# Two list fetches per slot instead of up to five in a row, and one if with an else at the end, in a fused attention and mixture-of-experts kernel

## The chip, the cores and the metric

The kernel runs on 1 core of one Trainium2 chip. The metric is the device time of one execution in microseconds (us). The engines are called as the profile calls them: PE (TensorE matmul), PEld (its weight load), DVE (VectorE), ACT (ScalarE), POOL (GpSimd) and SP (SyncE).

## The reference

Block-sparse attention over q, k and v of shape 4 x 8 x 768 x 64, then a mixture of eight experts in which each of the 3072 tokens goes to one expert:

```python
k_sum = k.reshape(B, H, nb, block, D).max(axis=3)          # 24 blocks of 32
v_sum = v.reshape(B, H, nb, block, D).mean(axis=3)
# softmax over the keys nearer than 16 and the 24 block sums (score + log 32)
a = softmax([local scores, summary scores])
x = (a @ [v, v_sum]) -> [3072, 512]
logits = x @ w_gate;  e_idx = argmax(logits)
for e in range(8):
    mask = e_idx == e
    ye = np.maximum(x[mask] @ w1[e], 0.0) @ w2[e]           # 512 -> 1024 -> 512
    out[mask] = gate_w[mask, None] * eom[mask, e, None] * ye
```

`gate_w` is the softmax probability of the chosen expert and `eom` the sigmoid of `x @ w_output_gate`.

## The kernel before, in words

**Attention and routing.** `attention` (L177) goes through 48 stages: 4 batches, 6 tiles of 128 tokens, 2 groups of 4 heads. PE transposes keys and queries, forms the scores (L329), transposes the probabilities (L347) and multiplies them with the values (L358); DVE and ACT do the softmax between them. Each finished tile `xs` of x (DVE, L368) is stored to DRAM (`x_dr`) by POOL (L371). When a batch is through, its 768 tokens are routed (L401 to L460): DVE works out for every token its expert, its weight and its place in that expert's list, and POOL scatters the pairs (token number, weight) into the lists in DRAM, `l_dr`, with six indirect DMAs for each batch, one for each tile (L456). Every scatter is remembered in `rt["scatters"]`.

**Slots.** The experts' lists are cut into slots of 256 tokens of one expert. For a slot POOL issues three kinds of indirect DMAs, two of each (128 tokens each):

- the *list fetch* (`fetch_list` L751, issued at L757) brings 256 pairs from `l_dr` into a tile of its own. It waits for all scatters that were issued up to then;
- the *row fetch* (`fetch` L765, L770) gathers the rows of x that the list names into the tiles `xg`, of which there are only two, so it can start when PE has transposed the rows of the slot before;
- the *write* (`write` L923; DVE L929, ACT L931, POOL L932) scatters the scaled results to the output.

`take_x` (L794) transposes the rows (PE L803) and splits them into two parts of lower precision (ACT L805, DVE L806). `first` (L813) is the first layer, 8 times 12 matmuls (L821 to L823), then ReLU and split (L824, L825). `second` (L913) is the second layer, 8 blocks of 6 matmuls (L909 to L911); ahead of its fifth block it takes the rows of the next slot and issues the row fetch of the one after. `fetch_w` (L774) loads the weights of the next slot (SP L789) and splits them (ACT L791, DVE L792). `half` (L855) handles a slot of 128 tokens.

**Order of the slots.** Three *early* slots (e0, e1, e2) hold tokens of the first two batches only. At stage 41 of 48 `start` (L835) fetches the lists of all three and the rows of e0. After the last stage `early` (L843) takes those rows, fetches the rows of e1 and computes the first layer of e0 between the parts of the last batch's routing, whose six scatters come there. Then come the second layer of e0, which fetches the rows of e2, `rest_slots` (L655, DVE: the tables of all further slots), the list of w0, and `run` (L938) with the seven slots e1, e2, w0 to w4:

```python
later = [("w", x) for x in range(1, SURE + 3)] + [("l", x) for x in range(3)]
for s in range(1, EARLY + SURE):
    for x in later[:4]:
        self.fetch_list(x, 2)
    del later[:4]
    self.full(*order[s:s + 3])
```

SURE is 5, so `later` has ten lists: four ahead of slot e1, four ahead of e2, two ahead of w0. From the second layer of e0 to the end of `run` POOL's order is the one in which the program is written (L139 to L147); elsewhere POOL, and everywhere PE, DVE and ACT, are ordered by a planner that simulates the program's time, except where a function writes the order by hand (SP in attention, PE in `half`).

`rest` (L948) handles what depends on the data. It loads three counts into registers: pairs, full slots left, half slots left. `more_pairs` (L958) is a chain of ifs, each of which fetches two lists (w8 and w9 in the first) and then does a full slot and a half slot. Then `more_full` (L969) and `more_half` (L978) are two chains of ifs, one behind the other, with one list fetched at the start of each slot. Every engine that takes part tests the condition for itself. With the data here there are three pairs, one full slot left and no half slot left, 12 full and 3 half slots in all. So the tests at L972 (one more full slot) and at L981 (a half slot) come last, and both fail.

Of the kernel before, what the change touches and what calls it, by code (L numbers as in the profile page):

```python
# [45 lines left out]
TB = S // P  # L46
# [3 lines left out]
EARLY = 3  # L50
# [6 lines left out]
NWOV = SURE + 2 * PAIRS + 2  # L57
NLEFT = max(MOST - SURE, E) + 2
# [575 lines left out]
def early_slots(tc, const, c_sb, rt):  # L634

    nc = tc.nc
    base = c_sb[:, C_BASE:C_BASE + E]
    t = const.tile([P, E], F32, name="t_early")
    ti = const.tile([P, E], I32, name="ti_early")
    nc.vector.tensor_tensor(ti, rt["base"], base, ALU.subtract)  # L640
    nc.vector.tensor_scalar(ti, ti, 8, None, ALU.logical_shift_right)
    nc.vector.tensor_copy(t, ti)
    inc = up_to(tc, const, "a", t)
    slots, exc = slot_tables(tc, const, c_sb, "a", c_sb[:, C_SLOT:C_SLOT + EARLY], t, inc, base, True)

    early = const.tile([P, E], F32, name="early")
    capped = const.tile([P, E], F32, name="capped")
    nc.vector.tensor_scalar(early, inc, float(EARLY), None, ALU.min)
    nc.vector.tensor_scalar(capped, exc, float(EARLY), None, ALU.min)
    nc.vector.tensor_tensor(early, early, capped, ALU.subtract)  # L650
    rt["early"] = early
    return slots


def rest_slots(tc, const, c_sb, rt, moe):  # L655
# [56 lines left out]
class Experts:  # L712
# [49 lines left out]
                                                                       mybir.DependencyReason.DATA))  # L762
        self.lists[s] = lst

    def fetch(self, s, n):  # L765

        nc = self.tc.nc
        rows = FIRST * S if s[0] == "e" else N
        for t in range(n):
            nc.gpsimd.indirect_dma_start(out=self.xg[t], out_offset=None, in_=self.x_dr[0:rows, :],  # L770
                                         in_offset=bass.IndirectOffsetOnAxis(ap=self.lists[s][:, t, 0:1], axis=0),
                                         bounds_check=rows - 1, oob_is_err=False)

    def fetch_w(self, which, s, tiles):  # L774

# [50 lines left out]
        if j % 4 == 3:  # L826
            self.fetch_w(1, nxt, range(j - 3, j + 1))

    def full(self, s, nxt, nxt2, nxt_n=2):
        hidden = self.hidden()  # L830
        for j in range(NF):
            self.first(j, hidden, nxt, "S" if j % 2 else "PT")
        self.second(s, 2, *hidden, nxt, nxt2, nxt_n, 2)

    def start(self, late_work):  # L835

        for s in range(EARLY):
# [75 lines left out]
    def second(self, s, n, hh, hl, nxt, nxt2, nxt_n, nxt2_n):  # L913
# [24 lines left out]
    def run(self):  # L938

        order = [("e", s) for s in range(EARLY)] + [("w", x) for x in range(SURE + 2)]  # L940
        later = [("w", x) for x in range(1, SURE + 3)] + [("l", x) for x in range(3)]
        for s in range(1, EARLY + SURE):
            for x in later[:4]:
                self.fetch_list(x, 2)
            del later[:4]
            self.full(*order[s:s + 3])

    def rest(self, counts):  # L948
        nc = self.tc.nc
        n_pairs = nc.values_load(counts[0:1, 0:1], min_val=0, max_val=PAIRS)  # L950
        n_full = nc.values_load(counts[0:1, 1:2], min_val=0, max_val=MOST - SURE)
        n_half = nc.values_load(counts[0:1, 2:3], min_val=0, max_val=E)
        self.more_pairs(0, n_pairs)
        self.more_full(0, n_full)
        self.expert.clear()
        self.more_half(0, n_half)

    def more_pairs(self, k, n):  # L958
        if k == PAIRS:
            return  # L960
        with self.tc.If(n > k):  # L961
            x = SURE + 2 * k
            for y in range(x + 3, min(x + 5, NWOV)):
                self.fetch_list(("w", y), 2)
            self.full(("w", x), ("w", x + 1), ("w", x + 2), 1)
            self.half(("w", x + 1), ("w", x + 2), ("w", x + 3), 2)
            self.more_pairs(k + 1, n)

    def more_full(self, x, n):  # L969
        if x == MOST - SURE:  # L970
            return
        with self.tc.If(n > x):  # L972
            if x + 3 < NLEFT:
                self.fetch_list(("l", x + 3), 2)
            self.full(*(("l", x + y) for y in range(3)))
            self.more_full(x + 1, n)

    def more_half(self, x, n):  # L978
        if x == E:
            return  # L980
        with self.tc.If(n > x):  # L981
# [30 lines left out]
```

## Time and profile before

| | |
|---|---|
| three runs | 580.85, 588.73, 586.81 us, median 586.81 us |
| the profiled execution | 576.87 us, of which the span is 575.0 us |
| mean granted clock of PE | 0.946 |
| busy, share of the span | PE 89%, PEld 77%, DVE 69%, ACT 59%, POOL 34% |
| DMA | 117.97 MB, mean 205 GB/s |
| POOL's row fetches of the later slots (L770) | 26 issues, 1084 ns each |

The span is the time from the first to the last instruction of the profiled execution. The slices of the profile cut the span into 40 equal parts of 14.4 us; a digit is the busy share in tenths, and PEclk is the clock that PE was granted, in tenths of full speed. A row of an engine's order of time gives start, duration, engine, line, operation, tiles, and in brackets how long the engine idled before it and what ended that idle time. A row of a table by stretches gives for each engine the busy time and the count of its instructions. Attention takes the first 230 us or so, the early slots follow up to about 290 us, then come the slots w0 to w4, the pairs from 432 us on, and the tail from 530 us.

### The profile page before, as it was taken

The page shows a single profiled execution, that of the slowest core. Times are in us where ns is not written, and L with a number is a line of the kernel's source. Part 1 is how long each engine was busy: PE and PEld are TensorE (multiplying, and loading weights), DVE is VectorE, ACT ScalarE, POOL GpSimd, SP SyncE. Part 2 cuts the span into 40 slices and gives each one's busy share as a digit, 9 for nine tenths or more (in the row PEclk, how much of TensorE's full clock was granted, in tenths as well). Part 3 has the DMA queues.
Part 4 walks back from the last instruction along what each step waited for, and adds up shares of the span by engine and source line. Part 5 has one row for each costly group of instructions (what it writes and reads, how often), then busy time and mean ns, then how long its engine had stood idle before and what let it go on. Part 6 is the DMA issues. An engine that isn't in the chain of part 4 may idle for free. (4 is left out here: it accounts for less than half of the span.)

```text
span 575.0 us, 12298 instructions
## 1 busy us (share of the span) xinstructions
PE 510.0 (89%) x3880; PEld 441.4 (77%) x3880; DVE 395.4 (69%) x1242; ACT 337.5 (59%) x752; POOL 193.5 (34%) x225
## 2 busy tenths in 40 slices
PE   6599997998879799897899999999999999998890
PEld 5598876786668587686789989989887887886870
DVE  7888896797758668594367576665767677578470
ACT  4388774785678556163356565554656567468360
POOL 6045355445242400736542211311232411512220
PEclk8699999899899699978899999999999999999896
DMA  9999999995928548592748476584566786576641
GB/s 249 210 241 279 215 245 221 208 242 142 166 64 256 160 174 292 66 273 73 238 147 274 142 269 222 182 305 154 218 218 224 257 295 233 190 282 224 186 142 28
DMA packets 117051, 117.97 MB, mean 205 GB/s; under 512 B 53787, under 2 KB 78651, under 8 KB 116192
## 3 DMA queue, kind: packets, MB, share of 16 engines
q1 hardware_dynamic: 107584, 97.02, 60.3%
q0 software_dynamic: 9376, 19.91, 10.8%
q8 instruction: 36, 0.59, 0.5%
q14 instruction: 55, 0.45, 0.2%
HBM read 106.30 MB, written 13.79 MB: 209 GB/s over the span
## 5 line engine op out<-in xcount | busy, mean ns | idle before, releaser
L821 PE MATMUL hp<-xhl,w1h 128*128 128x256 f32 x384 | 111.9, 295 | 7.1 <-DVEq L961 3.8
L822 PE MATMUL hp<-xhl,w1h 128*128 128x256 f32 x384 | 112.9, 295 | 4.1 <-issue 3.1
L823 PE MATMUL hp<-xhl,w1l 128*128 128x256 f32 x384 | 111.9, 292 | 2.6 <-issue 2.6
L909 PE MATMUL yp<-w2h,hh 128*128 128x512 f32 x216 | 87.6, 406 | 2.2 <-ACT hh L824 0.8
L911 PE MATMUL yp<-w2h,hl 128*128 128x512 f32 x216 | 85.9, 399 | 0.8 <-issue 0.4
L910 PE MATMUL yp<-w2l,hh 128*128 128x512 f32 x216 | 85.5, 396 | 0.9 <-issue 0.9
L821 PEld LDWEIGHTS hp<-xhl,w1h 128*128 128x128 f32 x384 | 76.8, 201 | 11.2 <-issue 9.3
L822 PEld LDWEIGHTS hp<-xhl,w1h 128*128 128x128 f32 x384 | 77.2, 201 | 8.1 <-issue 5.1
L825 DVE SCALAR_TENSOR_TENSOR hl<-hp,hh 128x256 fp32r<-128x256 f32 x96 | 39.2, 421 | 59.0 <-ACT hh L824 41.1
L824 ACT ACTIVATE hh<-hp 128x256 fp32r<-128x256 f32 x96 | 35.4, 381 | 74.6 <-PE hp L823 60.7
L823 PEld LDWEIGHTS hp<-xhl,w1l 128*128 128x128 f32 x384 | 77.2, 201 | 2.0 <-issue 2.0
L770 POOL DMA_INDIRECT xg<-x_dr,lst_w x26 | 28.2, 1084 | 141.2 <-PE xp L803 136.9
L339 ACT ACTIVATE pr<-sm,mn 128x120 f32<-128x120 f32 x192 | 61.9, 387 | 16.6 <-DVE mn L337 15.2
L329 PE MATMUL sp<-kt,qt 128*128 128x120 f32 x384 | 54.6, 287 | 6.6 <-DVE kt L304 6.5
L337 DVE CUSTOM_DVE_ANT_0 sm<-sp,c_sb 128x120 f32<-128x120 f32 x192 | 42.8, 277 | 20.6 <-remote 9.1
L329 PEld LDWEIGHTS sp<-kt,qt 128*128 128x128 f32 x384 | 49.7, 201 | 9.2 <-issue 7.8
L909 PEld LDWEIGHTS yp<-w2h,hh 128*128 128x128 f32 x216 | 41.1, 190 | 12.4 <-ACT hh L880 1.9
L911 PEld LDWEIGHTS yp<-w2h,hl 128*128 128x128 f32 x216 | 40.8, 190 | 11.6 <-DVE hl L881 1.6
L910 PEld LDWEIGHTS yp<-w2l,hh 128*128 128x128 f32 x216 | 41.0, 190 | 7.8
L347 PE MATMUL pt<-id_sb,pr 128*120 128x128 f32 x192 | 40.8, 301 | 4.0 <-issue 1.5
L358 PE MATMUL pv<-vw,pT 120*64 120x65 f32 x768 | 36.2, 232 | 7.9 <-ACT pT L200 3.2
L358 PEld LDWEIGHTS pv<-vw,pT 120*64 120x64 f32 x768 | 28.8, 140 | 16.5 <-issue 7.5
(735 smaller groups left out, 1042.2 us busy)
## 6 DMA issues: line engine op xcount, KB each, us to landing
vw<-in_v_dram SPq DMA_DIRECT2D x88, 96.0 KB
raw_k<-in_k_dram SPq DMA_DIRECT2D x12, 512.0 KB
raw_q<-in_q_dram SPq DMA_DIRECT2D x12, 512.0 KB
vm<-in_v_dram SPq DMA_DIRECT2D x8, 768.0 KB
x_dr<-xs POOLq DMA_DIRECT2D x24, 256.0 KB
vw<-vs_dr SPq DMA_DIRECT2D x36, 48.0 KB
vw<-in_v_dram SPq DMA_DIRECT2D x8, 64.0 KB
xg<-x_dr,lst_w POOLq DMA_INDIRECT x26
```

Source lines behind the costliest of these rows:

```text
L329: nc.tensor.matmul(sp[:, 2 * x + y, 0:W], lhsT=qt[:, 2 * g + x, li, :], rhs=kt[:, 2 * g + x, blk * KW:blk * KW + W], start=True, stop=True)
L337: nc.vector.tensor_tensor_reduce(out=sm[:, c, :], in0=sp[:, c, 0:W], in1=c_sb[:, m:m + W], scale=1.0, scalar=3.0e38, op0=ALU.add, op1=ALU. ...
L339: nc.scalar.activation(pr[:, c, :], sm[:, c, :], AF.Exp, bias=mn[:, c:c + 1], scale=-1.0)
L347: nc.tensor.transpose(pt[:, c, :], pr[:, c, :], id_sb)
L358: nc.tensor.matmul(po[64 * y:64 * y + 64, 2 * x + hh, :], lhsT=pT[:, 2 * x + y, 64 * hh:64 * hh + 64], rhs=VW[(NB * b + 2 * tok + y) % VR] ...
L821: nc.tensor.matmul(hp, lhsT=w_h[:, fs], rhs=self.xh[:, c, :], start=c == 0, stop=False)
L822: nc.tensor.matmul(hp, lhsT=w_h[:, fs], rhs=self.xl[:, c, :], start=False, stop=False)
L823: nc.tensor.matmul(hp, lhsT=w_l[:, fs], rhs=self.xh[:, c, :], start=False, stop=c == NC - 1)
L825: nc.vector.scalar_tensor_tensor(hl[:, j, :], hp, 0.0, hh[:, j, :].bitcast(F32), ALU.max, ALU.subtract)
L909: nc.tensor.matmul(y, lhsT=hh[:, j, tk], rhs=w_h, start=j == 0, stop=False)
L910: nc.tensor.matmul(y, lhsT=hh[:, j, tk], rhs=w_l, start=False, stop=False)
L911: nc.tensor.matmul(y, lhsT=hl[:, j, tk], rhs=w_h, start=False, stop=j == NF - 1)
```

## The change

- `start` fetches the lists of e0 and e1 only. The list of e2 is fetched in `early`, behind the row fetch of e1.
- `run` hands two lists to each `full`: the first is fetched at the slot's start, the second in `second`, right behind the row fetch. The ten lists go to the slots e1, e2, w0, w1 and w2.
- The row fetch of e2 is ordered behind the last six scatters: an order on POOL's queue, with no semaphore.
- In a pair the first list is fetched at the start of its full slot as before, the second between the full and the half slot.
- `rest` ends with one if and an else: a left full slot and all further ones, or else the half slots. `left_full` is the body of `more_full` with the list handed to `full`. The else starts from the expert numbers that SP had loaded ahead of the if (`seen`), where before all were forgotten (`self.expert.clear()`).

```diff
-    def fetch(self, s, n):
+    def fetch(self, s, n, behind=()):
...
+            for x in behind:
+                self.tc.add_manual_dep(i.ins, x.name, mybir.DependencyInfo(mybir.DependencyClass.NoSync,
+                                                                           mybir.DependencyReason.SCHED_ONLY))
...
-    def full(self, s, nxt, nxt2, nxt_n=2):
+    def full(self, s, nxt, nxt2, nxt_n=2, lists=()):
+
+        for x in lists[:1]:
+            self.fetch_list(x, 2)
         hidden = self.hidden()
         for j in range(NF):
             self.first(j, hidden, nxt, "S" if j % 2 else "PT")
-        self.second(s, 2, *hidden, nxt, nxt2, nxt_n, 2)
+        self.second(s, 2, *hidden, nxt, nxt2, nxt_n, 2, lists[1:])
 
     def start(self, late_work):
 
-        for s in range(EARLY):
+        for s in range(2):
             self.fetch_list(("e", s), 2)
...
         self.fetch(("e", 1), 2)
+        for s in range(2, EARLY):
+            self.fetch_list(("e", s), 2)
...
                 self.take_x(nxt_n)
-                self.fetch(nxt2, nxt2_n)
+                self.fetch(nxt2, nxt2_n, self.rt["scatters"][-TB:] if nxt2[0] == "e" else ())
+                for x in lists:
+                    self.fetch_list(x, 2)
...
         for s in range(1, EARLY + SURE):
-            for x in later[:4]:
-                self.fetch_list(x, 2)
-            del later[:4]
-            self.full(*order[s:s + 3])
+            self.full(*order[s:s + 3], lists=later[:2])
+            del later[:2]
...
-        self.more_full(0, n_full)
-        self.expert.clear()
-        self.more_half(0, n_half)
+
+        seen = dict(self.expert)
+        with self.tc.If(n_full > 0) as left:
+            self.left_full(0)
+            self.more_full(1, n_full)
+        self.expert = seen
+        with left.Else():
+            self.more_half(0, n_half)
...
-            for y in range(x + 3, min(x + 5, NWOV)):
-                self.fetch_list(("w", y), 2)
-            self.full(("w", x), ("w", x + 1), ("w", x + 2), 1)
+            lists = [("w", y) for y in range(x + 3, min(x + 5, NWOV))]
+            self.full(("w", x), ("w", x + 1), ("w", x + 2), 1, lists[:1])
+            for y in lists[1:]:
+                self.fetch_list(y, 2)
```

More of the change, by code (lines that the diff above doesn't have):

```diff
@@ L769, in fetch @@
         for t in range(n):
-            nc.gpsimd.indirect_dma_start(out=self.xg[t], out_offset=None, in_=self.x_dr[0:rows, :],
-                                         in_offset=bass.IndirectOffsetOnAxis(ap=self.lists[s][:, t, 0:1], axis=0),
-                                         bounds_check=rows - 1, oob_is_err=False)
+            i = nc.gpsimd.indirect_dma_start(out=self.xg[t], out_offset=None, in_=self.x_dr[0:rows, :],
+                                             in_offset=bass.IndirectOffsetOnAxis(ap=self.lists[s][:, t, 0:1], axis=0),
+                                             bounds_check=rows - 1, oob_is_err=False)
+            for x in behind:
+                self.tc.add_manual_dep(i.ins, x.name, mybir.DependencyInfo(mybir.DependencyClass.NoSync,
+                                                                           mybir.DependencyReason.SCHED_ONLY))
     def fetch_w(self, which, s, tiles):
@@ L911, in second_block, with second @@
             nc.tensor.matmul(y, lhsT=hl[:, j, tk], rhs=w_h, start=False, stop=j == NF - 1)
-    def second(self, s, n, hh, hl, nxt, nxt2, nxt_n, nxt2_n):
+    def second(self, s, n, hh, hl, nxt, nxt2, nxt_n, nxt2_n, lists=()):
         yp = [self.ps.tile([P, DM], F32, name=f"yp{t}", tag="PV", bufs=PB["PV"]) for t in range(n)]
@@ L972, in more_full, with left_full @@
         with self.tc.If(n > x):
-            if x + 3 < NLEFT:
-                self.fetch_list(("l", x + 3), 2)
-            self.full(*(("l", x + y) for y in range(3)))
+            self.left_full(x)
             self.more_full(x + 1, n)
+    def left_full(self, x):
+        self.full(*(("l", x + y) for y in range(3)), lists=[("l", x + 3)] if x + 3 < NLEFT else [])
     def more_half(self, x, n):
```

## The prediction

> **What bounds the kernel now.** I read the page's slices first, then busy time by stretches, then TensorE (PE) in order of time, then GpSimd (POOL) in order of time.
>
> ```profile
> PE   6599997998879799897899999999999999998890
> PEclk8699999899899699978899999999999999999896
> ```
>
> PE is the engine to watch: in the second half 16 slices in a row are at 9 or more. Just before, in the slices from 244 to 287 us (one slice is 14.4 us), its granted clock is down to 7 and 8 tenths. In stretches (columns: PE, PEld, DVE, ACT, POOL busy with counts, granted clock, DMA share, GB/s):
>
> ```profile
> 157.00:163.00 6.00, 3.10 (x29) 2.86 (x26) 0.33 (x4) 1.48 (x3) 5.03 (x7) 1.00 0.30 69
> ...
> 252.00:262.50 10.50, 10.50 (x56) 8.85 (x55) 7.89 (x22) 4.57 (x9) 8.18 (x8) 1.00 0.79 282
> 262.50:270.00 7.50, 3.43 (x17) 2.56 (x17) 1.60 (x4) 1.75 (x3) 3.93 (x4) 0.84 0.21 50
> 270.00:281.00 11.00, 11.00 (x70) 10.66 (x70) 6.35 (x17) 4.67 (x11) 8.35 (x8) 0.80 0.64 204
> 281.00:288.00 7.00, 4.87 (x17) 3.46 (x16) 2.84 (x6) 3.31 (x8) 1.91 (x2) 0.76 0.59 205
> ...
> 290.15:313.60 23.45, 23.45 (x153) 21.35 (x152) 15.64 (x28) 13.54 (x27) 8.44 (x8) 1.00 0.60 194
> ```
>
> In 290.15 to 313.60 PE has no gap: a slot at its floor. In 262.5 to 270 and 281 to 288 it runs 17 matmuls each, every other engine but POOL idles too, and DMA is far from full. The steps of the slots are read off the transposes that take a slot's rows (one take_x per slot; two records of the second are missing):
>
> ```profile
> 228.87 1.36 PE L803 MATMUL xp<-id_sb,xg 128*128 128x128 f32 x8 [0.56 <-DVE at L432]
> ...
> 254.76 0.81 PE L803 MATMUL xp<-id_sb,xg 128*128 128x128 f32 x6
> ...
> 290.15 1.03 PE L803 MATMUL xp<-id_sb,xg 128*128 128x128 f32 x8
> ...
> 313.64 1.03 PE L803 MATMUL xp<-id_sb,xg 128*128 128x128 f32 x8
> ```
>
> A clean slot is 313.64 - 290.15 = 23.49 us. The step before it took 35.39 (11.90 lost), the one before that 25.89 (2.40 lost). The lost time is no wait for a named engine:
>
> ```profile
> 267.28 0.38 PE L821 MATMUL hp<-xhl,w1h 128*128 128x256 f32 x1 [1.12 <-issue]
> ```
>
> "issue" means that nothing which the profile shows was late. What stands beside these gaps is POOL's row of indirect DMAs:
>
> ```profile
> 252.15 1.00 POOL L757 DMA_INDIRECT lst_w<-l_dr,rowib  x1 [8.50 <-DVE hsc L628]
> ...
> 264.02 0.95 POOL L757 DMA_INDIRECT lst_w<-l_dr,rowib  x1 [0.30 <-issue]
> 265.28 1.02 POOL L770 DMA_INDIRECT xg<-x_dr,lst_w  x1 [0.30 <-issue]
> 266.60 1.00 POOL L770 DMA_INDIRECT xg<-x_dr,lst_w  x1 [0.30 <-issue]
> 270.49 1.22 POOL L932 DMA_INDIRECT out_dram<-y,lst_e  x1 [2.89 <-DVE y L929]
> ...
> 282.53 0.95 POOL L757 DMA_INDIRECT lst_l<-l_dr,rowid  x1 [0.30 <-issue]
> 291.35 1.25 POOL L770 DMA_INDIRECT xg<-x_dr,lst_w  x1 [7.87 <-PE xp L803]
> ...
> 297.16 1.22 POOL L932 DMA_INDIRECT out_dram<-y,lst_e  x1 [3.25 <-DVE y L929]
> ...
> 303.91 0.95 POOL L757 DMA_INDIRECT lst_l<-l_dr,rowid  x1 [0.30 <-issue]
> ```
>
> Ten list fetches and two row fetches from 252.15 to 267.60 without a break: PE falters from 262.5 to 270. Two writes and eight list fetches from 270.49 to 283.48: PE falters again from 281. Two writes and four list fetches from 297.16 to 304.86: nothing. I read a long unbroken row of POOL's indirect DMAs as what starves every engine towards its end. That is an inference from place and time; no view names the mechanism.
>
> **The change, part by part.** The sum is made against the profiled execution (576.87 us, span 575.0) and then carried to the median, 586.81; the profiled one was 1.7% below that median and below all three timed runs, so only the difference is carried over.
>
> *The second row in run().* The lists of slots 1 and 2 came in fours (eight DMAs); now two lists come per slot, one ahead of its first half and one behind its row fetch, and the row from 270.49 falls apart. Its share of the 11.90 us, an estimate: PE's idle time in 281 to 288, 7.00 - 4.87 = 2.13, and for the clock 0.24 x 7.00 = 1.68, together 3.8. The first row's, likewise: 4.07 + 0.16 x 7.50 + 0.20 x 11.00 = 7.5. The 0.6 left over is shared: 4.1 and 7.8. Value -4.1; bounds -4.1 and 0.
>
> *The first row.* It gets no shorter in count: lists w0 (2 DMAs), w1 (2), rows of w0 (2), list w2 (2), then the slot's writes (2; due about 7 us behind its take_x, as 297.16 is behind 290.15, so at 262) and list w3 (2) follow with nothing between, again 12 from 252.15 on, some 16 us. What changes is that no more than four list DMAs stand together. Bounds: 0 (the count decides) and -7.8 (list DMAs in a row decide: four behind two writes, 297.16 to 304.86, cost nothing). Neither row is nearer, so I take less than half, -3.0.
>
> *New rows of eight.* In three slots (e2, w0, w1) the DMAs are now rows 2, list 2, writes 2, list 2, nearly unbroken: the 3.25 us between rows and writes is filled by two issues of 1.3 us (11.87 us for nine steps from 252.15 to 264.02). The clean slot from 290.15 also carried eight, spread over 13.5 us, at no cost; a pair's eight in a row cost a little:
>
> ```profile
> 451.17 1.05 POOL L770 DMA_INDIRECT xg<-x_dr,lst_w  x1 [10.02 <-PE xp L803]
> ...
> 460.62 1.02 POOL L770 DMA_INDIRECT xg<-x_dr,lst_w  x1 [0.30 <-issue]
> 462.86 0.28 PE L823 MATMUL hp<-xhl,w1l 128*128 128x256 f32 x1 [1.02 <-issue]
> ```
>
> (The last is from PE's order of time.) So 0 to 3 x 1.0 = +3.0; nearer the clean slot, +0.8. In the pairs the second list moves behind full(), but POOL's order there is the planner's, and neither list waits for anything: 0, bounds -3.0 (three such gaps) and 0.
>
> *start().* Two of six list DMAs leave the row from 153.99 (the third line is from DVE's order of time):
>
> ```profile
> 153.99 1.00 POOL L757 DMA_INDIRECT lst_e<-l_dr,rowia  x1 [2.60 <-DVE xs L368]
> ...
> 160.39 0.95 POOL L757 DMA_INDIRECT lst_e<-l_dr,rowia  x1 [0.30 <-issue]
> 162.76 0.28 DVE L337 CUSTOM_DVE_ANT_0 sm<-sp,c_sb 128x120 f32<-128x120 f32 x1 [5.67 <-remote]
> ```
>
> DVE stood 5.67 us, until 1.4 us after the sixth list. A step is 6.40 / 5 = 1.28 us, so two fewer may end the standstill 2.6 us sooner. Attention's stages share PE, DVE and ACT, so I take -2.0; bounds -2.9 (PE's idle time in 157 to 163, 6.00 - 3.10) and 0.
>
> *Slot 2's list in early().* Its two DMAs now follow slot 1's rows and hold back one store of x:
>
> ```profile
> 196.45 1.04 POOL L770 DMA_INDIRECT xg<-x_dr,lst_e  x1 [0.30 <-issue]
> 198.48 0.61 POOL L371 DMA_DIRECT2D x_dr<-xs  x1 [0.99 <-DVE xs L368]
> ```
>
> The list also waits for the third batch's scatters. The store queued behind it feeds a row fetch that comes at 257 at the earliest, a cover of some 55 us. Only the longer row counts: 0 to +2.6, I take +0.8.
>
> *Rows of slot 2 behind the last scatters.*
>
> ```profile
> 230.40 1.07 POOL L770 DMA_INDIRECT xg<-x_dr,lst_e  x1 [21.76 <-PE xp L803]
> 231.77 1.03 POOL L456 DMA_INDIRECT l_dr<-pair,posi  x1 [0.30 <-DVE inc1b L586]
> ...
> 238.69 0.97 POOL L456 DMA_INDIRECT l_dr<-pair,posi  x1 [0.30 <-issue]
> 239.97 1.05 POOL L770 DMA_INDIRECT xg<-x_dr,lst_e  x1 [0.30 <-issue]
> ```
>
> The scatters start up to 1.4 us sooner; the first row fetch goes from 230.40 to about 238.6, the second stays. Both are taken at 254.76: cover 14.8 us. Without it the price would be the first fetch's 8.2 us. The row of ten stays ten, so the 2.40 lost there stays. Sooner scatters let the lists of 252.15 go sooner, but the rows behind them are needed only at 290.15: 0. Bounds -1.4 and +1.4.
>
> *The end.*
>
> ```profile
> L972 ACTq EVENT_SEMAPHORE  x1: 17/17/17, 564.0 to 564.0; - x1
> L981 ACTq EVENT_SEMAPHORE  x1: 17/17/17, 568.1 to 568.1; - x1
> L981 POOLq INC_SWDGE_SEM  x1: 1360/1360/1360, 567.4 to 567.4; - x1
> L952 POOLq TENSOR_LOAD <-counts x1: 294/294/294, 566.5 to 566.5; - x1
> ```
>
> The path here (one left full slot, no left half) passes two tests that fail, L972 and L981. Afterwards the second is a jump over the else. POOL ends its part at 567.4 + 1.36 = 568.8; without load, test and count it would end up to 2.6 sooner, but ACT comes to 568.1 less a load and a test, some 567.6. So -1.1; the half count's load may move ahead of the if on PE, +0.3. Value -0.8; bounds -2.6 and +1.4 (one more count of POOL's for the other branch). [...]
>
> **Sum.** -4.1 - 3.0 + 0.8 + 0 - 2.0 + 0.8 + 0 - 0.8 = -8.3 us: 568.6 for a profiled execution, 586.8 - 8.3 = 578.5 for the median, 1.4% faster.
>
> **Rivals.** *A, list DMAs in a row are all that starves.* Then the first row goes too, and new eights cost nothing: -4.1 - 7.8 - 2.6 - 0.8 = -15.3, 571.5 us, faster by 2.6%. For it: four lists cost nothing, eight and ten did. Against it: a pair's eight, only four of them lists, had a gap of 1.02.
> *B, the rows are innocent.* The gaps have another cause and stay; only the end is left, -0.8, 586.0 us. For it: the profile names no releaser, and the first row keeps its twelve. Against it: the gaps lie at the ends of such rows, and there are none in 290.15 to 313.60. [...]
> *C, slower.* The interleaved order makes a starving row in every slot: rows, list, writes, list without a break of 3 us. If eight suffice to cost what the first row cost, the price is 7.8 in each of three slots, +23.4, less the second row's 4.1 and start's 2.0: +17.3, 604.1 us. It is slower at all from 2.3 us a slot (6.9 / 3). For it: the first row runs on into list w3. Against it: a pair's eight cost 1.02.
> *D, it does not do what it says.* Twelve in a row stay, and three eights at 1.0 eat most of the second row's gain: -4.1 + 3.0 - 0.8 = -1.9, 584.9 us.
>
> **How the numbers follow.** Forecast 0.47, A 0.23, B 0.14, C 0.06, D 0.10. The range goes from A with 2.5 us to spare, 569, to B and D with as much as the median's runs lie above it (2 us) and the bounds of the small terms, 590; C and more than A's gain are left out. Faster by over 2% (below 575.1; about what a measurement of this kernel tells from no change) is A and a little of the forecast: 0.25. Slower by over 2% (above 598.5) is most of C: 0.05. Same: 0.70.
>
> **What would show it.** Right: the steps between take_x transposes are about 26, then 28 to 33 (before: 35.39), then 23.5 to 24.5; PE has no "issue" gaps around 281; DVE's standstill after the first lists ends by 160.5; POOL's second INC_SWDGE_SEM at the end is gone. Wrong: a step of 35 again (B), of 24 (A), or 26 and more in each of the next slots (C). What I could not see is how the planner, which orders attention by simulated time, shifts other instructions as two list fetches leave its start; a few us there would spoil the sum without touching its terms.

## The result, and the profile after

| | before | after |
|---|---|---|
| median of 6 runs | 582.91 us (580.03 to 588.73) | 562.27 us (553.75 to 565.99) |
| the profiled execution | 576.87 us, span 575.0 us | 562.20 us, span 560.4 us |

The ratio is 0.954, with a 95% interval of 0.944 to 0.965: faster. It is made over the runs of each kernel that lie within 1.5% of its fastest, which leaves out four of the six after, the profiled one (562.20 beside 553.75) among them. The plain medians give 562.27 / 582.91 = 0.965, at the edge of the interval. The forecast was 578.5 us, 1.4% faster, and its range began at 569: too high by 16 us. Of these, 3.9 come from the base, since the kernel before had a median of 586.81 us over three runs and of 582.91 over six. By the medians the change brings 20.6 us, by the two profiled executions 14.7 us, against 8.3 forecast.

The page of the kernel after, PE's slices and its granted clock (one slice is 14.0 us now):

```profile
PE   6599998899799699889999999999999999999790
PEclk8699998899899879979999999999999999999896
```

Of the slices with a lower clock from 244 to 287 us one 7 is left (238 to 252 us, the scatters); behind it clock and PE stand at 9 up to the tail. The take_x transposes of the slots (PE's order of time, kernel after, now L807):

```profile
228.49 1.36 PE L807 MATMUL xp<-id_sb,xg 128*128 128x128 f32 x8 [0.56 <-DVE at L432]
...
254.34 1.04 PE L807 MATMUL xp<-id_sb,xg 128*128 128x128 f32 x8
...
278.70 1.03 PE L807 MATMUL xp<-id_sb,xg 128*128 128x128 f32 x8
...
302.19 1.03 PE L807 MATMUL xp<-id_sb,xg 128*128 128x128 f32 x8
```

The steps are 25.85 (before 25.89), 24.36 (before 35.39) and 23.49 (before 23.49). So 11.03 of the 11.90 us that slot e2 lost are back. POOL's row there, kernel after, the first and the last of its twelve, then the first and the last of the next eight:

```profile
249.82 1.20 POOL L757 DMA_INDIRECT lst_w<-l_dr,rowib  x1 [6.54 <-DVE which L705]
...
265.78 0.97 POOL L757 DMA_INDIRECT lst_w<-l_dr,rowib  x1 [0.30 <-issue]
279.90 1.30 POOL L771 DMA_INDIRECT xg<-x_dr,lst_w  x1 [13.14 <-PE xp L807]
...
289.85 0.96 POOL L757 DMA_INDIRECT lst_w<-l_dr,rowic  x1 [0.31 <-issue]
```

and the engines in the same stretches (columns as in the prediction's table):

```profile
235.00:246.00 11.00, 7.62 (x41) 5.90 (x40) 3.08 (x13) 2.23 (x7) 6.45 (x7) 0.88 0.94 153
249.80:262.00 12.20, 12.20 (x67) 10.48 (x67) 12.00 (x34) 8.25 (x16) 9.74 (x9) 0.98 0.64 220
262.00:270.00 8.00, 7.55 (x62) 7.25 (x61) 3.23 (x11) 2.72 (x7) 3.84 (x4) 1.00 0.20 68
270.00:281.00 11.00, 11.00 (x68) 9.69 (x67) 7.66 (x16) 7.23 (x17) 1.10 (x1) 1.00 0.91 314
```

Twelve indirect DMAs stand in a row as before, and PE is busy 12.20 of 12.20 and 7.55 of 8.00 us beside them, at a granted clock of 0.98 and 1.00. They are further apart than before: (265.78 - 249.82) / 11 = 1.45 us a step, where the twelve before took (266.60 - 252.15) / 11 = 1.31. Only the stretch from 235 to 246, where the scatters run, still falters.

Where the rest of the 14.6 us of span came from shows in POOL's scatters. First the kernel before, first scatter of the second and of the third batch:

```profile
136.09 1.01 POOL L456 DMA_INDIRECT l_dr<-pair,posi  x1 [0.30 <-DVE t_early L642]
...
183.70 1.04 POOL L456 DMA_INDIRECT l_dr<-pair,posi  x1 [1.68 <-DVE mn L337]
```

then the kernel after:

```profile
138.84 1.00 POOL L456 DMA_INDIRECT l_dr<-pair,posi  x1 [0.30 <-DVE t_early L642]
...
183.13 1.03 POOL L456 DMA_INDIRECT l_dr<-pair,posi  x1 [1.82 <-DVE mn L337]
```

Up to the second batch's scatters the change touches nothing, and this execution was 2.75 us later there, which I put down to chance: in the other traces from these slower chips (7, 2 and 14, see below) that scatter starts between 136.8 and 140.9 us. Between the two scatters lies `start`: 44.29 us instead of 47.61, 3.3 less. That is one pair of executions: seven traces with the new start from those chips and from the result have 43.75 to 48.41 us there, three with the old one 47.61 to 49.68. DVE's standstill behind the first lists is half as long (DVE's order of time, kernel after; before 5.67):

```profile
162.43 0.28 DVE L337 CUSTOM_DVE_ANT_0 sm<-sp,c_sb 128x120 f32<-128x120 f32 x1 [2.77 <-PE xtr L377]
```

At the end the second test is gone from POOL, and ACT comes sooner (instructions of L987, kernel after):

```profile
L987 ACTq EVENT_SEMAPHORE  x1: 17/17/17, 551.1 to 551.1; - x1
L987 POOLq INC_SWDGE_SEM  x1: 1377/1377/1377, 552.7 to 552.7; - x1
```

From POOL's last write to the span's end: 560.4 - 549.65 = 10.8 us, before 575.0 - 561.12 = 13.9, so 3.1 less. Sum: +2.75 - 3.3 - 11.0 - 3.1 = -14.7, and nothing is left for the pairs.

### The profile page after: what moved, and what is told of

It reads as the page before. It is cut to its first block, busy times and chain, and to the rows that moved or that the text cites. A ratio compares the mean times of both kernels' runs of the same rounds, so it can differ in the third digit from the quotient of the medians.

```text
span 560.4 us, 12263 instructions
## 1 busy us (share of the span) xinstructions
PE 505.5 (90%) x3880; PEld 438.5 (78%) x3880; DVE 396.3 (71%) x1242; ACT 336.6 (60%) x752; POOL 195.7 (35%) x225
## 3 DMA queue, kind: packets, MB, share of 16 engines
q0 software_dynamic: 9376, 19.91, 10.8%
## 5 line engine op out<-in xcount | busy, mean ns | idle before, releaser
L827 PE MATMUL hp<-xhl,w1l 128*128 128x256 f32 x384 | 110.7, 289 | 1.0 <-issue 1.0
L825 PEld LDWEIGHTS hp<-xhl,w1h 128*128 128x128 f32 x384 | 75.9, 199 | 8.4 <-issue 6.1
L826 PEld LDWEIGHTS hp<-xhl,w1h 128*128 128x128 f32 x384 | 76.2, 199 | 4.9 <-DVE xhl L810 2.3
L329 PE MATMUL sp<-kt,qt 128*128 128x120 f32 x384 | 55.9, 292 | 6.5 <-DVE kt L304 6.5
L329 PEld LDWEIGHTS sp<-kt,qt 128*128 128x128 f32 x384 | 51.0, 205 | 8.9 <-issue 7.8
L918 PEld LDWEIGHTS yp<-w2h,hh 128*128 128x128 f32 x216 | 40.7, 188 | 13.4 <-ACT hh L889 2.7
L920 PEld LDWEIGHTS yp<-w2h,hl 128*128 128x128 f32 x216 | 40.5, 188 | 10.8 <-DVE hl L890 1.6
L358 PE MATMUL pv<-vw,pT 120*64 120x65 f32 x768 | 36.4, 232 | 3.8 <-DVE pT L196 1.8
L358 PEld LDWEIGHTS pv<-vw,pT 120*64 120x64 f32 x768 | 28.7, 140 | 13.0 <-issue 5.7
```

The lines of the kernel that those rows point to most:

```text
L329: nc.tensor.matmul(sp[:, 2 * x + y, 0:W], lhsT=qt[:, 2 * g + x, li, :], rhs=kt[:, 2 * g + x, blk * KW:blk * KW + W], start=True, stop=True)
L358: nc.tensor.matmul(po[64 * y:64 * y + 64, 2 * x + hh, :], lhsT=pT[:, 2 * x + y, 64 * hh:64 * hh + 64], rhs=VW[(NB * b + 2 * tok + y) % VR] ...
L825: nc.tensor.matmul(hp, lhsT=w_h[:, fs], rhs=self.xh[:, c, :], start=c == 0, stop=False)
L826: nc.tensor.matmul(hp, lhsT=w_h[:, fs], rhs=self.xl[:, c, :], start=False, stop=False)
L827: nc.tensor.matmul(hp, lhsT=w_l[:, fs], rhs=self.xh[:, c, :], start=False, stop=c == NC - 1)
L918: nc.tensor.matmul(y, lhsT=hh[:, j, tk], rhs=w_h, start=j == 0, stop=False)
```

## The experiments

**A first surprise: one chip on which nothing is lost.** Four kernels, each with one part undone or done alone, ran beside the kernel before on one chip.

*u_run*: the list fetches of run() put back.

```diff
-            self.full(*order[s:s + 3], lists=later[:2])
-            del later[:2]
+            for x in later[:4]:
+                self.fetch_list(x, 2)
+            del later[:4]
+            self.full(*order[s:s + 3])
```

> The changed kernel with only the list fetches of run() put back (four, four and two at the starts of slots 1 to 3). Theory, that the long rows of list fetches starve all engines: the step of slot e2 goes from 24.4 back to about 35 us, and the time is about 11 us above the changed kernel's, so 9 to 10 us below the kernel before. Rival, that the gain of that step comes from the sooner scatters or from the list of e2 being fetched later: the step stays near 24 us and the time stays within 2 us of the changed kernel's.

*u_start*: the three early lists in a row again.

```diff
-        for s in range(2):
+        for s in range(EARLY):
             self.fetch_list(("e", s), 2)
...
-        for s in range(2, EARLY):
-            self.fetch_list(("e", s), 2)
```

> The changed kernel with the three early lists fetched in a row again (six list DMAs in start, none in early). Theory: DVE's standstill around the sixth list comes back, some 2.9 us between the scatters of the third batch and the first rows, and the rest stays; about 3 us above the changed kernel, too little for the timed runs to tell but to be read off the trace. Rival, that start was no part of it: scatters to first rows takes the same as in the changed kernel (24.1 us from the first scatter of that batch to the first row fetch).

*u_end*: two ifs in a row again.

```diff
-        seen = dict(self.expert)
-        with self.tc.If(n_full > 0) as left:
-            self.left_full(0)
-            self.more_full(1, n_full)
-        self.expert = seen
-        with left.Else():
-            self.more_half(0, n_half)
+        self.more_full(0, n_full)
+        self.expert.clear()
+        self.more_half(0, n_half)
```

> The changed kernel with two ifs in a row at the end. Theory, that POOL's own chain of load, test and count is what ends last: from POOL's last write to its final drain takes 7.9 us again instead of 4.9, and the span is 2.7 to 3.1 us longer. Rival, that ACT's jump sets the end: no more than 1 us longer.

*o_run*: the kernel before with run()'s part alone (the reverse of u_run's diff, and full() and second() with the lists handed through).

> The kernel before with only the list fetches of run() spread, two to a slot. Theory: the step of slot e2 falls from 35.4 to about 24.4 us, and the time is some 11 us (1.9 per cent) below the kernel before; start's and the end's stalls stay. Rival, that the rows matter only together with the sooner scatters: the step stays above 30 us.

On this chip (number 11) the kernel before took 554.14 us (549.89 to 560.04), not 583. The four took 551.58 (ratio 0.998, 0.993 to 1.002), 550.84 (0.994, 0.990 to 0.999), 553.89 (0.999, 0.994 to 1.004) and 555.56 us (1.000, 0.995 to 1.005). Neither my theory nor the rivals had room for that: with nearly the old rows in place there was nothing to win. The step of e2 in u_run is 24.36 us there, with the lists of run() put back. POOL's row in u_run on chip 11, thirty indirect DMAs without a break (the first, the fifteenth and the last):

```profile
243.41 1.00 POOL L757 DMA_INDIRECT lst_w<-l_dr,rowib  x1 [4.30 <-DVE pastc L604]
...
263.54 0.99 POOL L757 DMA_INDIRECT lst_w<-l_dr,rowic  x1 [0.30 <-issue]
...
284.10 0.95 POOL L757 DMA_INDIRECT lst_l<-l_dr,rowid  x1 [0.30 <-issue]
```

and the engines beside it:

```profile
252.00:264.00 12.00, 12.00 (x95) 11.66 (x94) 9.01 (x25) 5.59 (x13) 9.56 (x9) 1.00 0.37 107
269.00:281.00 12.00, 12.00 (x80) 10.91 (x79) 8.44 (x15) 7.00 (x15) 9.26 (x10) 1.00 0.76 258
```

PE does not falter at all, although the last sixteen are (284.10 - 263.54) / 15 = 1.37 us apart. The traces of chip 11 also decide on the two small parts. The end is there: from POOL's last write to the span's end u_end takes 13.4 us, u_run and u_start, with the new end, 10.9 and 11.1. The start is not: DVE's wait behind the early lists is 4.34 us with six lists in a row (u_start, o_run) as with four (u_run), and it ends with PE's scores; what was expected of u_start did not come. Four more, the changed kernel itself among them, fell on chip 11 again:

> The changed kernel itself once more, beside the next three on one chip, since two chips showed two times for the kernel before (554 us and 583 us). If this chip is of the kind on which the kernel before takes some 583 us: 0.95 to 0.97 of it. If it is of the kind with 554 us, where the traces show almost no stalls: 0.99 to 1.00, the end's 2.7 us (0.5 per cent) alone.

> The changed kernel with only the list fetches of run() put back, as before in u_run. On a chip where the kernel before takes some 583 us, theory: the step of slot e2 is about 35 us again and the time 11 us above the changed kernel's. Rival: the step stays near 24 us. On a chip with 554 us: no difference.

> The kernel before with only the list fetches of run() spread. On a chip where the kernel before takes some 583 us, theory: the step of slot e2 is about 24 us and the time 11 us below the kernel before. Rival: the step stays near 35 us. On a chip with 554 us: no difference.

> The changed kernel with a break of about 1.5 us on POOL (16 small memsets) after the third of each batch's six scatters, after the last batch's sixth, and between the rows of e2 and the writes of e0. Theory, that any indirect DMAs starve the engines when some nine stand closer than about 1.4 us: on a chip where the kernel before takes some 583 us the steps of e0 and e1, together 25.9 us from take to take, fall by 3 to 5 us, and the time lies 3 to 6 us below the changed kernel's. Rival, that only list fetches do it: no gain, or up to 2 us of loss for the later scatters. On a chip with 554 us: same within 2 us.

Kernel before 553.54 us; after_b 551.93 (0.998, 0.995 to 1.001), u_run_b 553.24 (0.998, 0.995 to 1.001), o_run_b 553.60 (0.998, 0.993 to 1.002), paced 555.56 (1.005, 1.001 to 1.008). So on chip 11 the change is worth at most 0.5%, which the timed runs can't tell from nothing. On the chips 7, 2 and 14, where the rest ran, the kernel before took 582.79 (one run), 582.86 and 580.24 us, as in the comparison that the result rests on. The changed kernel itself was not run beside them there. What follows speaks of them.

**Run()'s part, undone and done alone.**

> The changed kernel with only the list fetches of run() put back, a third time. On a chip where the kernel before takes some 583 us, theory: the step of slot e2 is about 35 us again and the time some 572 to 575 us. Rival: the step stays near 24 us, the time near 562 us. On a chip with 554 us: no difference, as twice before.

Chip 2: 572.32 us beside 582.86 (0.987, 0.979 to 0.996, a gain of 2% is not certain), with start and end of the changed kernel kept. Its take_x rows:

```profile
250.68 1.03 PE L807 MATMUL xp<-id_sb,xg 128*128 128x128 f32 x8
...
287.36 1.03 PE L807 MATMUL xp<-id_sb,xg 128*128 128x128 f32 x8
```

The step of e2 is 36.68 us: theory right, rival out. POOL's row in u_run_c (the first, the twelfth, the last of 22) and the engines:

```profile
248.61 1.21 POOL L757 DMA_INDIRECT lst_w<-l_dr,rowib  x1 [6.44 <-DVE which L705]
...
264.89 1.46 POOL L771 DMA_INDIRECT xg<-x_dr,lst_w  x1 [0.30 <-PE hp L827]
...
278.19 0.95 POOL L757 DMA_INDIRECT lst_l<-l_dr,rowid  x1 [0.30 <-issue]
```

```profile
252.00:264.00 12.00, 12.00 (x81) 10.97 (x80) 10.43 (x31) 4.56 (x10) 9.56 (x9) 1.00 0.28 92
...
269.00:281.00 12.00, 5.48 (x15) 2.96 (x14) 0.42 (x1) 0.39 (x1) 7.71 (x9) 0.75 0.76 270
```

The kernel and the stretches are those of u_run above (its row began 5.2 us earlier), and there PE was busy 12.00 of 12.00 us in the second one. What starves is therefore not in the program alone. Here the first twelve, 1.48 us apart, cost nothing, though ten of them are list fetches in a row; the next ten, (278.19 - 264.89) / 10 = 1.33 us apart, stop everything:

```profile
275.53 0.37 PE L827 MATMUL hp<-xhl,w1l 128*128 128x256 f32 x1 [1.03 <-issue]
```

> The kernel before with only the list fetches of run() spread. On a chip where the kernel before takes some 583 us, theory: the step of slot e2 is about 24 us and the time some 571 to 573 us. Rival, that the rows only matter together with the sooner scatters: the step stays above 30 us. On a chip with 554 us: no difference.

Chip 14: 562.77 us beside 580.24 (0.973, 0.965 to 0.980, a gain of 2% is just not certain). The take_x rows of o_run_c:

```profile
255.31 0.82 PE L803 MATMUL xp<-id_sb,xg 128*128 128x128 f32 x6
...
278.57 1.03 PE L803 MATMUL xp<-id_sb,xg 128*128 128x128 f32 x8
```

The step is 23.26 us, without sooner scatters, without the change of start. Run()'s part alone carries most of the gain. The time is 17.5 us below the kernel before, more than the 11 to 12 us of that step, and below the 571 to 573 us expected; no trace of the kernel before was taken on chip 14, so where the other 6 us lie is open.

**Start and end on such a chip.**

> The changed kernel with the three early lists in a row again. On a chip where the kernel before takes some 583 us, theory: DVE's standstill after the lists comes back and the time is some 565 us, 3 us above the changed kernel's 562. Rival, that the early list in early() is the costly place and start brought nothing: 560 to 562 us. On a chip with 554 us: no difference.

> The changed kernel with two ifs in a row at the end. On either kind of chip, theory: POOL's end takes 2.7 us longer, some 565 us where the kernel before takes 583. Rival: no difference in the tail.

Chip 14: 560.93 us (0.966, 0.957 to 0.974) and 558.22 us (0.962, 0.955 to 0.970). The times expected were some 565 us, so both missed, and the time of u_start_c is the rival's: a part of 3 us is below what the timed runs can tell. The traces tell both. In u_start_c DVE stands

```profile
166.88 0.28 DVE L337 CUSTOM_DVE_ANT_0 sm<-sp,c_sb 128x120 f32<-128x120 f32 x1 [5.78 <-remote]
```

again, 3.0 us longer than after. In u_end_c POOL counts twice again (L982 and L992), and the second count (the first stands ahead of it),

```profile
L982 POOLq INC_SWDGE_SEM  x1: 1377/1377/1377, 550.4 to 550.4; - x1
L992 POOLq INC_SWDGE_SEM  x1: 1360/1360/1360, 553.1 to 553.1; - x1
```

comes 2.7 us behind; from the last write to the end it takes 13.5 us (after 10.8; 11.2 in u_start_c on the same chip).

**What of the rows starves.** Extra indirect DMAs whose data nobody reads were put into the slots w3 and w4 of the changed kernel, which took 23.49 us each:

```diff
         for j in range(NF):
             self.first(j, hidden, nxt, "S" if j % 2 else "PT")
+            if j == 0 and s in EXTRA:
+                self.extra(s, hidden[0])
...
+    def extra(self, s, hh):
...
+        nc.gpsimd.tensor_copy(gate, hh[:, 0, 0:1].bitcast(F32))
+        for k in range(EXTRA[s]):
...
+            i = nc.gpsimd.indirect_dma_start(out=lst, out_offset=None, in_=self.l_dr,
...
```

> The changed kernel with extra list fetches whose result nobody reads, in two slots that took 23.49 us: 8 in an unbroken row in slot w3 and 12 in w4, started once the first block of the first layer is done. Theory (rows of small DMAs starve all engines once they are some nine long): w3 takes 23.5 to 25.5 us, w4 some 28 to 32 us, with gaps on PE that no wait explains. Rival, that a row alone does nothing and the place in the program made the stalls: both stay within 0.5 us of 23.49.

> As the run with extra list fetches, but each extra fetch brings 256 bytes to a partition instead of 8 (128 pieces of x). Theory with count alone: the same steps as with the 8-byte lists, w4 28 to 32 us. Theory with small pieces (only list-like DMAs starve): both steps within 1 us of 23.49.

> Twelve extra list fetches in w3 and w4 both: in w3 with a memset of about 1 us on POOL behind each, in w4 in threes of four with a memset of about 4 us behind each four. Theory, that the density counts: both steps within 1 us of 23.49, though as many lists are fetched as in the row of twelve. Rival, that the count of list fetches in a slot decides: both some 28 to 32 us like the unbroken twelve.

Chip 7, one profiled execution each, the take_x rows of w3, w4 and the slot behind. lad_list:

```profile
347.11 1.03 PE L808 MATMUL xp<-id_sb,xg 128*128 128x128 f32 x8
...
379.49 1.03 PE L808 MATMUL xp<-id_sb,xg 128*128 128x128 f32 x8
...
413.38 1.03 PE L808 MATMUL xp<-id_sb,xg 128*128 128x128 f32 x8
```

lad_256:

```profile
344.39 1.03 PE L809 MATMUL xp<-id_sb,xg 128*128 128x128 f32 x8
...
377.24 1.03 PE L809 MATMUL xp<-id_sb,xg 128*128 128x128 f32 x8
...
406.27 1.03 PE L809 MATMUL xp<-id_sb,xg 128*128 128x128 f32 x8
```

lad_gap:

```profile
345.09 1.03 PE L809 MATMUL xp<-id_sb,xg 128*128 128x128 f32 x8
...
369.47 1.03 PE L809 MATMUL xp<-id_sb,xg 128*128 128x128 f32 x8
...
393.04 1.03 PE L809 MATMUL xp<-id_sb,xg 128*128 128x128 f32 x8
```

| | w3 | w4 |
|---|---|---|
| lad_list, 8 and 12 unbroken | 32.38 | 33.89 |
| lad_256, 8 and 12 unbroken, 256 bytes each | 32.85 | 29.03 |
| lad_gap, 12 with a memset (0.55 us) behind each, 12 in fours with one of 1.83 us behind each four | 24.38 | 23.57 |

The rows starve with 256-byte pieces of x as with 8-byte lists, so the size and the kind of the DMA do not decide whether they starve (the expectation of at most 1 us for it is out); twelve of 256 bytes cost 5.5 us instead of 10.4, in one execution each. Twelve lists with breaks cost 0.9 and 0.1 us, so the number in a slot does not decide either. Eight cost nearly as much as twelve, where 2 us at most were expected. The row of w3 is longer than I had meant: the rows, lists and writes of w2 run into it, fourteen in all,

```profile
349.74 1.02 POOL L772 DMA_INDIRECT xg<-x_dr,lst_w  x1 [12.65 <-PE yp L937]
...
366.60 0.95 POOL L852 DMA_INDIRECT xl<-l_dr,rowib  x1 [0.30 <-issue]
```

(366.60 - 349.74) / 13 = 1.30 us apart, and beside its last part PE, DVE and ACT stand while DMA is nearly empty:

```profile
360.00:368.00 8.00, 3.24 (x21) 2.89 (x20) 1.54 (x3) 1.75 (x4) 5.71 (x7) 0.90 0.02 1
```

> The run with 8 and 12 extra list fetches again. On a chip where the kernel before takes some 554 us: if the chip decides whether a row starves, both steps stay within 1 us of 23.49. If the extra row starves the engines on every chip and chip 11 only has spare room, the steps are again some 32 to 34 us. On a chip with 583 us: 32 to 34 us as before.

On chip 2 it came out like on chip 7: 32.27 and 34.99 us. What the same rows cost on chip 11 was not measured.

**Breaks in the scatters.** *paced* and *paced_c* put 16 small memsets on POOL behind the third scatter of a batch, behind the last batch's sixth, and behind the rows of e2; *paced2* has five, and none in the third batch nor behind the rows. From paced2:

```diff
+def pause(tc, rt, others):
...
+    for _ in range(PAUSE):
+        i = tc.nc.gpsimd.memset(rt["pause"], 0.0)
+        behind(tc, i, others)
...
+            if t >= 3 and b != 2:
+                behind(tc, i, last)
             rt["scatters"].append(i.ins)
+            if t == 2 and b != 2:
+                last = pause(tc, rt, [i.ins])
```

> The changed kernel with breaks of about 1.5 us in the rows of scatters, again. On a chip where the kernel before takes some 583 us, theory (every kind of indirect DMA counts): 3 to 6 us below the changed kernel's. Rival (list fetches alone): 0 to 3 us above it. On a chip with 554 us: 2 us above the kernel before, as measured there.

> The changed kernel with short breaks on POOL (five small memsets, about 1 us) after the third scatter of batches 0, 1 and 3 and after the last scatter. On a chip where the kernel before takes some 583 us, theory (scatters starve as lists do, and a short break is enough): the gaps at 234 to 244 us are gone and the time is 558 to 561 us, below the changed kernel's 562. Rival, that the break costs in later rows what it saves, as the longer breaks did: 562 to 566 us. On a chip with 554 us: 0 to 1 us above the kernel before.

paced_c took 564.93 us on chip 2 (0.969, 0.962 to 0.977), where 3 to 6 us less than the changed kernel's 562 were expected. Its 16 memsets take 3.3 us and not 1.5; rows, writes and lists of the next slots then stand in a new row of eighteen with two short breaks, and PE falters beside it (7.94 of 9.00 us from 259 to 268). paced2 took 558.02 us on chip 14 (0.963, 0.955 to 0.970), the same as u_end_c there; the changed kernel itself was not run beside it, so whether paced2 beats it is open. What the trace of paced2 does show is the stretch of the scatters:

```profile
235.00:246.00 11.00, 11.00 (x82) 10.37 (x82) 10.01 (x55) 4.45 (x10) 8.41 (x17) 1.00 0.56 73
```

PE 11.00 of 11.00 us, where the kernel after had 7.62: beside the unbroken row of scatters there PE falters as beside rows of lists, and with the short breaks in this trace it does not. The step of e1 is 21.42 us, beside 25.85 in the kernel after and 24.12 to 26.42 in the three other traces from chip 14, and then PE waits for data:

```profile
254.88 0.41 PE L829 MATMUL xp<-id_sb,xg 128*128 128x128 f32 x2 [2.55 <-DMA xg<-x_dr,lst_e]
```

Its time does not show these 3 to 5 us. The end takes 13.8 us in this trace, as long as before the change, though there is one count only: POOL reaches its final drain 2.5 us behind the test, in the kernel after 0.35. So the saving at the end did not come in every trace of a kernel that has it.

## Why the prediction was wrong, point by point

- **The first row: the step that failed.** I wrote that it "gets no shorter in count", twelve again, and took "less than half, -3.0" of 7.8. The term was mis-sized. Both rows together were worth 11.0 (e2's step 35.39 to 24.36; 36.68 with run()'s part undone, 23.26 with it alone), so the first row, still twelve long, gave up all of its share. My bound of -7.8 held; my choice inside it was wrong. Count was the wrong measure: of two rows of twelve, the one before starved and the one after did not.
- **What to put in its place** is shown in part. With breaks in the row most of the loss is gone (lad_gap: 0.9 and 0.1 us left, where lad_list lost 8.9 and 10.4; paced2: PE busy 11.00 of 11.00 us beside the scatters). The spacing sorts the long rows on the starving chips: ten or more stop the engines at 1.26 to 1.36 us a step (before 1.31, u_run_c's second part 1.33, lad_list 1.30 and 1.26, the scatters with rows and writes 1.36 before and 1.35 after), and twelve at 1.45 (after) or 1.48 (u_run_c's first part) do not. But the spacing is partly an effect. In the kernel before the nine DMAs ahead of the first standstill (263.2; PE, DVE and ACT all idle for over 0.3 us) were 1.33 us apart. In u_run_c the fourteen ahead of it (269.3) were 1.49 apart and the eight behind it 1.27, while DVE did next to nothing (0.42 of 12.00 us); where DVE was busy (10.43 of 12.00 us from 252 to 264), five of POOL's eleven issues up to 264 took 1.21 to 1.73 us, where the last six of the row took 0.95 or 0.96. Ten lists and two rows in a row starved in the kernel before and not in u_run_c. So that spacing alone decides is not shown. Nor is ten a threshold: beside rows of six scatters in attention PE, DVE and ACT stand together for 0.47 to 0.89 us at a time in the kernel before and 0.41 to 1.12 in the kernel after. At the pv matmuls (L358) PE's idle time that ends in "issue" is 2.6 us in the kernel before; in u_run on chip 11 it is at most 0.4, out of 1.1 us of idle time there. In the kernel before, behind the scatter at 136.09 (PE's order of time):

```profile
141.91 0.29 PE L358 MATMUL pv<-vw,pT 120*64 120x65 f32 x2 [1.15 <-issue]
...
143.36 0.40 PE L394 MATMUL lt<-c_sb,ls 128*128 128x16 f32 x3 [0.89 <-issue]
```

- **The second row**, -4.1: its loss is gone. The runs can't tell its share from the first row's.
- **New rows of eight**, +0.8: slot e2 has 24.36 - 23.49 = 0.87 left; in o_run_c (23.26) and u_end_c (23.49, with the same rows) there is nothing. So between nothing and the forecast, 0.8.
- **Start**, -2.0: the direction is right. DVE stood 5.67 to 5.88 us with six lists in a row (before, u_start_c, o_run_c) and less with four (2.77 in the kernel after, up to 4.85 in lad_list). The size is 2.9 by DVE's standstill (5.67 to 2.77) and 3.3 by the scatters, at or just past the bound of -2.9, with the spread named above. The early list, +0.8, would fall between the third batch's scatters and the take_x that follows: 45.17 us before, 45.36 after, so 0.2 at most.
- **Rows behind the last scatters**, 0: the number came, by another way than I wrote. I took two transposes of e2's rows for missing records. They are in the trace, ahead of the others (PE's order of time, kernel before):

```profile
236.33 0.38 PE L803 MATMUL xp<-id_sb,xg 128*128 128x128 f32 x2
```

  So the first row fetch had no cover up to 254.76, and its new place, 238.26, lies behind this use. The planner moved these two to the others (all eight at 254.34 now), and the step stayed (25.89 and 25.85). I had not seen that; that it cost nothing was luck.
- **Pairs**, 0: as forecast; from w0's take_x to POOL's last write it is 270.97 us before and 270.95 after.
- **The end**, -0.8: 3.1 in the profiled execution. I had ACT end things at 567.6, 6.5 us behind POOL's last write. It comes sooner as well: ACT and POOL reach their final drain 4.8 and 4.9 us behind that write, before 7.1 and 7.9, so POOL's whole second round (load, test, count: 2.7 us in u_end_c) is saved, a little past the bound that I had named. In paced2 the time is not won, as said above.
- **From profile to median.** The terms above, corrected, give -11.0 - 3.3 - 3.1 = -17.4 for a profiled execution, which a later start of the second batch's scatters made 14.7. My sum had -8.3: of the 9.1 missing, some 4.7 are the first row's, 2.3 the end's, 1.3 start's and 0.8 the early list's. The other 3 us up to 20.6 lie within the spread of the runs (553.75 to 565.99 for the kernel after).
- **The rivals.** A's time (571.5) came nearest, but its reason, that list DMAs in a row are all that starves, is out: pieces of x and scatters starve too, and ten lists in a row in u_run_c's first part did not. B and D are out by u_run_c and o_run_c, C by the steps of 23.49. The runs show stalls of every engine beside POOL's DMAs on some chips (PE busy 5.48, DVE 0.42 and ACT 0.39 of 12.00 us in u_run_c) and none on another (PE 12.00 of 12.00 in u_run); by what way a row stops the engines they do not show.

**What stays open: the mechanism.** What differs between the chips shows in the trace itself. Counted from the traces, records of semaphore updates by DMA engines:

| | chip | records | time |
|---|---|---|---|
| u_run | 11 | 9215 | 549.77 us |
| after_b | 11 | 9218 | 555.98 us |
| before | not on record | 7247 | 576.87 us |
| after | not on record | 7309 | 562.20 us |
| u_run_c | 2 | 7288 | 570.84 us |
| o_run_c | 14 | 7443 | 562.39 us |
| lad_gap | 7 | 7210 | 560.76 us |

The traces from chip 11 have 9193 to 9226 of these records, all others 7198 to 7508, a fifth less, for the same DMAs or more; records of instructions are not missing (12263 in after as in after_b). In u_run (chip 11) the row from 257 to 270 us leaves 23 records of semaphore updates per us, by engines and DMAs together, besides 22 instructions per us, while a clean slot (290 to 313) leaves 17. In u_run_c, with the same row, 10 per us arrive beside its first twelve DMAs and 7 from 264 to 270, and then the engines stop. So the traces with the long stops are all among those that lack records, and my guess is that the recording of the profile has a part in the stops; no run shows it. Against it stands that records are missing where nothing stops: beside the row of twelve in the kernel after (249.8 to 265.8) 9.6 per us arrive with 20 instructions. If the recording is the cause, the loss belongs to it, and since every run here, timed ones too, comes with a recorded span and clock, an execution without recording may show neither the loss nor the gain. This is argued, not shown. That chip 11 itself differs is not shown either: its runs came in longer series (31 executions of the kernel before, 7 or fewer on the others), and what else differs beside it is not on record. Whether the higher rate of matmuls in the first layer matters (in the kernel before one starts every 0.12 us there, around 212 us, and every 0.23 in the second layer, around 218), where most of the stalls lie (8.0 of the 8.4 us of PE's idle time that ends in "issue" behind 250 us), was not tried, nor was the order of e2's rows by itself.

## What to carry to other kernels

Here idle times of PE, DVE and ACT at once (0.32 to 1.12 us each from 263 to 270 us in the kernel before) that ended in "issue" on PE were no property of the instructions that they stood at: slot w4's matmuls took 33.89 us beside an unbroken row (lad_list) and 23.57 beside a broken one (lad_gap). So look for what another engine does in a dense row there, and break the row up; here its count alone told little (twelve starved before, 1.31 us apart, and not after, 1.45 apart), and its spacing may be an effect of the stop. Before a gain of this kind is believed in general, run the kernel before on more than one chip: here the change is worth 3.5% (medians) to 4.6% where the kernel before takes 583 us, and 0.2%, no more than the noise, on the chip where it takes 554. Cut the tail by whole rounds of the slowest engine (load, test, count: 2.7 us for POOL's second one in u_end_c), not by the test alone, and look in a trace whether the saving came (10.8 us from the last write to the end in the kernel after, 13.8 in paced2, 13.9 before).

## What the runs showed of the hardware that was not expected

- The same kernel before takes 554 us on one chip and 580 to 583 us on three others. No trace of it from the first one exists; for u_run and u_run_c, one kernel on two chips, the median durations of the matmuls are the same (283 and 283 ns in the first layer, 393 and 394 in the second), and of the 21.1 us between the spans 12.3 lie in the step of e2.
- In the traces from chips 7 and 2 and in the two of the comparison, PE, ACT and DVE stop beside rows of ten or more of POOL's indirect DMAs 1.26 to 1.36 us apart: lists (PE busy 3.24 of 8.00 us in lad_list), pieces of x (4.44 of 9.00 in lad_256), scatters with rows and writes (7.62 of 11.00 in the kernel after). With a memset of 1.83 us after every four, a slot with twelve extra lists took 23.57 us (lad_gap, floor 23.49).
- Sixteen memsets of 128x64 on POOL took 3.3 us in a row, 0.2 us each (paced_c).
